# Linear attention and two expert layers on one core: the left pad of SBUF made 32 bytes shorter, and two block differences moved ahead

## The chip, the cores and the metric

The kernel runs on one core of a Trainium2 chip. A core has a matmul engine (PE, with its weight loads shown apart as PEld), a vector engine (DVE), a scalar engine (ACT), a GpSimd engine (POOL) and a sync engine (SP), which here issues nearly all DMAs. They share SBUF, 128 partitions wide; matmuls write to PSUM. The metric is the device time of one execution in microseconds (us), lower is better.

## The reference

```python
kv  = einsum('bhsd,bhse->bhde', k, v)              # B 4, H 8, S 576, D 64
out = einsum('bhsd,bhde->bhse', q, kv)             # linear attention
x   = out / sqrt(mean(out*out, -1) + 1e-6) * g_norm
x   = x.transpose(0, 2, 1, 3).reshape(2304, 512)
h   = x @ w_in                                      # 512 -> 2048
x   = (h * clip(h + 3, 0, 6) / 6) @ w_out           # 2048 -> 512
p   = domain_probs / (domain_probs.sum(-1, keepdims=True) + 1e-9)
y   = sum over e of p[:, e:e+1] * (relu(x @ w1[e]) @ w2[e])     # 4 experts, 512 -> 1024 -> 512
```

All inputs are float32. The weights of the first layer pass through a bit conversion on the way in (lines 144 to 162).

## The kernel before, in words

**Precision.** Matmul operands are float32r. Each float32 value is split into a high part (an ACT copy to float32r) and a low part (a DVE subtraction), and each product is made of three matmuls: high·high, high·low, low·high. Every matmul has a 128x128 stationary operand, loaded just before it.

**Three stages.** First the attention, in eight halves of a batch element. Then stage two, the first layer: 16 column tiles of the hidden dimension in units of 1, 2, 3, 4 and 6 tiles, and for each unit five token blocks, four of 512 tokens and one of 256. `ff_in` makes 12 matmuls that share a PSUM bank, with x as the moving operand (lines 333 to 335; high parts in tiles xh0 to xh4, low parts in xl0 to xl4). ACT and DVE make the activation of it and split it into gH and gL. `ff_out`, three steps behind, makes 12 matmuls with gH or gL as the moving operand (line 356). Four `ff_in` calls are used as filling in the attention already. The sums over units stand in acc.

Then stage three, the four experts, in three passes over 768 tokens each; a pass has 16 quads (4 experts times 4 pairs of hidden tiles). The product x @ w1 is made in 7 instead of 8 block products (Strassen's way), so each quad needs sums and differences of weight blocks (tile `sums`, lines 554 to 559, split into `win`) and each pass needs seven moving tiles xs1 to xs7 of 384 tokens: some are plain pieces of acc, others are differences, made in `st1` and `st2` (line 603) and then split (lines 543 and 544). `quad` makes the products 6, 2, 5, 7, 3, 4 of 6 matmuls each, 384 columns wide (line 656), in two PSUM banks in turn, x and y; the first product of the next quad follows. ACT and DVE take the four results c11, c12, c21, c22 from the banks, and split them with the ReLU into `g2`. c11 and c12 rest in `st1` in between, c22 and c21 in `cs`. `outs` of the quad before makes 36 matmuls, 512 columns wide, with `wout` as the moving and `g2` as the stationary operand (line 630), and DVE adds the result, times the token's probability, to acc2 (lines 644 and 646) after the last quad of an expert.

**What sets the order.** A scheduler of the framework orders each engine's instructions by data dependencies, from the order in which the program issues them; on the chip each engine then runs its own list in order. `ahead`, `side` and `builds` are lists of small pieces of ACT and DVE work that the program issues between matmuls: `ahead` before stage three, `side` between the 36 matmuls of line 630. The pieces of the next pass are split: xs1 goes into `side` of the last quad of a pass, the other six are `builds`, issued in the first quad of the next.

**Where the tiles lie.** Pools are laid out from the left end of SBUF and, with side="right", from the right end. Left: the constants and small tiles up to byte 4960 of a partition, then the left pad (48 float32, 192 bytes), then acc, gH and gL, r, xh3 to xl4, and behind them xh0 to xl2 in stage two, and `sums`, st1, st2 and xs1 to xs6 in stage three (xs3 and xs7 take the places of xh3 and xl3). All of these have sizes that are multiples of 512 bytes, so all start where the first does: at byte 5152, which is 32 more than a multiple of 512. A slice with which a matmul starts is a multiple of 512 bytes into its tile. Right: the right pad, the weight tiles of stage two, raw2, `wout`, `g2` and `win`; they start at multiples of 512 bytes.

Of the kernel before, what the change touches and what calls it, by code (L numbers as in the profile page):

```python
# [17 lines left out]
def kernel(  # L18
# [39 lines left out]
    TH = 384  # L58
# [3 lines left out]
    LAG = 3  # L62
    RATE = (4200, 3000, 2600, 2900, 0)
    FMAX = 3.0e38
    PADL, PADR = 48, 248

    const = ctx.enter_context(tc.tile_pool(name="const", bufs=1))
    sp = ctx.enter_context(tc.tile_pool(name="sp", bufs=1))
# [454 lines left out]
    sums = xsp.tile([P, 4, 2, P], F32, tag="sums", name="sums")  # L523
    st1 = xsp.tile([P, 2, TH], F32, tag="st1", name="st1")
    st2 = xsp.tile([P, 2, TH], F32, tag="st2", name="st2")
# [15 lines left out]
    def split(dst, src):  # L541

        nc.scalar.activation(out=dst[0], in_=src, func=AF.Copy)  # L543
        nc.vector.tensor_tensor(out=dst[1], in0=src, in1=dst[0].bitcast(F32), op=ALU.subtract)  # L544

    def convert_in(k):

        r = raw2[k][:, 0].rearrange("p (c i f) -> p i c f", c=KD, i=2)
        win[k] = w = winp.tile([P, 2, 7, 2, P], F32R, tag="win", name="win")
        a11, a12, a21, a22 = (r[:, i, 2 * c:2 * c + 2, :] for i in range(2) for c in range(2))  # L550
        split([w[:, y, 0:2].rearrange("p m c f -> p (m c) f") for y in range(2)], r[:, 0])
        yield
        split([w[:, y, 2] for y in range(2)], a22)
        nc.vector.tensor_tensor(out=sums[:, 0], in0=a21, in1=a22, op=ALU.add)
        yield
        nc.vector.tensor_tensor(out=sums[:, 1], in0=sums[:, 0], in1=a11, op=ALU.subtract)
        nc.vector.tensor_tensor(out=sums[:, 2], in0=a11, in1=a21, op=ALU.subtract)
        yield
        nc.vector.tensor_tensor(out=sums[:, 3], in0=a12, in1=sums[:, 1], op=ALU.subtract)
        split([w[:, y, 3:5] for y in range(2)], sums[:, 0:2])  # L560
        yield
        split([w[:, y, 5:7] for y in range(2)], sums[:, 2:4])
        yield

    def convert_out(k):

        r = raw2.pop(k)[:, 1].rearrange("p (f d) -> p f d", f=2)
        wout[k] = w = wp.tile(
            [P, 2, 2, DM], F32R, tag=f"w{(NA + len(ftiles) + 2 + k % 2) % NW}", name="wout")
        for f in range(2):  # L570
            split([w[:, f, y] for y in range(2)], r[:, f])
            if f == 1:
                load2(k + 2)
            yield

    def build(p):

        t1, t2 = PASSES[p]

        def pieces(h, c):  # L580
            return [(acc[b][:, 2 * c:2 * c + 2, o:o + n], slice(z, z + n)) for b, o, n, z in h]

        b11, b12, b21, b22 = pieces(t1, 0), pieces(t2, 0), pieces(t1, 1), pieces(t2, 1)

        def new(m):
            pool = xp if m in XSHOME else xsp
            xs[m] = pool.tile([P, 2, 2, TH], F32R, tag=XSHOME.get(m, f"xs{m}"), name=f"xs{m}")
            return xs[m]

        def plain(m, b):  # L590
            x = new(m)
            for s, z in b:
                split([x[:, y, :, z] for y in range(2)], s)

        def summed(m, dst, a, b):

            x = new(m)
            if not isinstance(a, list):
                a = [(a[:, :, z], z) for _, z in b]
            if not isinstance(b, list):  # L600
                b = [(b[:, :, z], z) for _, z in a]
            for (s, z), (s2, _) in zip(a, b):
                nc.vector.tensor_tensor(out=dst[:, :, z], in0=s, in1=s2, op=ALU.subtract)  # L603
            split([x[:, y] for y in range(2)], dst)

        return {
            1: lambda: plain(1, b11),
            5: lambda: summed(5, st1, b12, b11),
            6: lambda: summed(6, st2, b22, st1),
            2: lambda: plain(2, b21),  # L610
            3: lambda: plain(3, b22),
            7: lambda: summed(7, st1, b22, b12),
            4: lambda: summed(4, st1, b21, st2),
        }

    def outs(k):

        p, e, j = quads[k]
        w = wout.pop(k)
        g = g2.pop(k)  # L620
        if j == 0:
            po_t["e"] = [bank_b([P, DM], "po2") for _ in range(NI2)]
        ps = po_t["e"]
        lower, upper = range(NI2 // 2), range(NI2 // 2, NI2)
        for part, f in ((lower, 0), (upper, 0), (upper, 1), (lower, 1)):
            for i in part:
                t, o = divmod(i * P, TH)
                gH, gL = (g[f][:, y, t, o:o + P] for y in range(2))
                for m, (lhsT, y) in enumerate(((gH, 0), (gH, 1), (gL, 0))):
                    nc.tensor.matmul(  # L630
                        ps[i], lhsT=lhsT, rhs=w[:, f, y],
                        start=(j == 0 and f == 0 and m == 0), stop=(j == FP - 1 and f == 1 and m == 2))
                    yield
                if f == 1 and j == FP - 1:
                    finish(p, e, i, ps[i])
# [15 lines left out]
    def product(k, bank, m, first):  # L651
        n = 0
        w = win[k]
        for c in range(2):
            for wy, xy in ((0, 0), (0, 1), (1, 0)):
                nc.tensor.matmul(  # L656
                    bank, lhsT=w[:, wy, AOP[m], c], rhs=xs[m][:, xy, c],
                    start=first and n == 0, stop=n == 5, skip_group_check=True)
                n += 1

    def pair(k):
        return (qa, qb) if k % 2 == 0 else (qb, qa)

    def first_product(k):

        x, y = pair(k)
        product(k, x, 1, True)
        return lambda: nc.scalar.activation(out=y, in_=x, func=AF.Copy)

    def quad(k):  # L670


        x, y = pair(k)
        g2[k] = g = [
            wp.tile([P, 2, 2, TH], F32R, tag=f"w{(NA + len(ftiles) + 4 + 2 * (k % 2) + f) % NW}", name="g2")
            for f in range(2)]
        us = xp.tile([P, 2, TH], F32, tag="xh4", name="us")
        cs = xp.tile([P, 2, TH], F32, tag="xl4", name="cs")
        u2, u4, c22, c21, c11, c12 = (z[:, y] for z in (us, cs, st1) for y in range(2))

        def high(f, t, src, func=AF.Relu):
            nc.scalar.activation(out=g[f][:, 0, t], in_=src, func=func)  # L682

        def low(f, t, src):
            nc.vector.scalar_tensor_tensor(  # L685
                out=g[f][:, 1, t], in0=src, scalar=0.0, in1=g[f][:, 0, t].bitcast(F32),
                op0=ALU.max, op1=ALU.subtract)

        product(k, y, 6, False)
        nc.scalar.activation(out=u2, in_=y, func=AF.Copy)  # L690
        product(k, x, 2, False)
        nc.scalar.activation(out=c11, in_=x, func=AF.Copy)  # L692
        high(0, 0, c11)
        low(0, 0, c11)
        product(k, y, 5, False)
        nc.scalar.activation(out=u4, in_=y, func=AF.Copy)  # L696
        product(k, x, 7, True)
        nc.vector.tensor_tensor(out=c22, in0=x, in1=u4, op=ALU.add)  # L698
        high(1, 1, c22)
        low(1, 1, c22)  # L700
        product(k, y, 3, False)
        nc.scalar.activation(out=c12, in_=y, func=AF.Copy)
        high(0, 1, c12)
        product(k, x, 4, False)
        nc.vector.tensor_tensor(out=c21, in0=x, in1=u2, op=ALU.add)
        low(0, 1, c12)
        high(1, 0, c21)
        low(1, 0, c21)
        win.pop(k)

    def run(g):
        return lambda: next(g, None)
# [2 lines left out]
    load2(0)  # L715
    load2(1)
    first = build(0)
    ahead = [first[m] for m in (1, 5, 6, 2, 4)] + [run(convert_in(0))] * 5 + [run(convert_in(1))] * 5
    for n in range(N3 + 1, NI):
        step(n)  # L720
        if ahead:
# [13 lines left out]
    builds = []  # L735
    for k in range(NQ):
        last_of_pass = k + 1 < NQ and quads[k + 1][0] != quads[k][0]
        ci, co = convert_in(k + 1) if 0 < k and k + 1 < NQ else iter(()), convert_out(k)
        side = builds + [run(co), run(co)] + [run(ci)] * 5
        builds = []  # L740
        if last_of_pass:
            nxt = build(quads[k + 1][0])
            side.append(nxt[1])
            builds = [nxt[m] for m in (5, 6, 2, 7, 3, 4)]
        seed()
        every = -(-NI2 * 6 // len(side))
        for z, _ in enumerate(filler):
            if z % every == every - 1 and side:
                side.pop(0)()
        for x in side:  # L750
            x()
        quad(k)
        if k + 1 < NQ:
            seed = first_product(k + 1)
        filler = outs(k)
# [32 lines left out]
```

## Time and profile before

| | |
|---|---|
| profiled execution | 1240.69 us |
| its span, first to last instruction | 1238.8 us |
| runs | 1242.1, 1431.24 and 4258.09 us, median 1431.24 |
| PE busy | 1219.2 us, 98% of the span |
| DVE, ACT busy | 765.6 and 574.3 us, 62% and 46% |
| DMA | 87.14 MB, 70 GB/s in the mean |
| granted PE clock, mean | 0.997 |

The three runs lie far apart; the profiled execution stands beside the lowest of them, and the trace is of it. Busy time of PE counts each matmul from start to end, and matmuls overlap: what a matmul costs is the distance from its start to the next one's, which the chain of waits and the timeline show.

### The profile page before, as it was taken

Reading aid. Unit: us, or ns where it says so; the run is one execution under the profiler, and the core shown is the slowest. Engines: PE = TensorE matmul, PEld = TensorE weight load, DVE = VectorE, ACT = ScalarE, POOL = GpSimd, SP = SyncE. Lnnn points to the kernel's source line nnn. Section 1 sums busy time; section 2 is a strip of 40 time slices with the busy share of each in tenths; the row PEclk is TensorE's granted clock in tenths of the full one; section 3 lists DMA queues with packets and bytes.
Section 4 is the critical chain, followed back from the end, with each engine's and each line's share of the span. In section 5 each row is a group of like instructions: output and inputs, shape, how many; then the busy total and the mean of one; then the engine's idle time right before and its main releaser. Section 6 shows DMA issues by size and latency. Waiting matters only on the chain.

```text
span 1238.8 us, 17507 instructions
## 1 busy us (share of the span) xinstructions
PE 1219.2 (98%) x7069; PEld 1065.7 (86%) x7069; DVE 765.6 (62%) x1469; ACT 574.3 (46%) x1146; POOL 1.6 (0%) x13
## 2 busy tenths in 40 slices
PE   7899999999999999999999999999999999999998
PEld 5778888888888889999999989999999899999997
DVE  5989996673533555565656586656565866565643
ACT  6778453432422334444444454444444644444442
POOL 0000000000000000000000000000000000000000
PEclk8999999999999999999999999999999999999999
DMA  9812221110010001221122122121111221112101
GB/s 336 261 54 86 69 85 34 36 50 1 27 43 1 1 1 68 69 68 68 69 69 68 69 85 102 69 68 69 66 66 67 77 96 67 66 65 68 67 34 51
DMA packets 60832, 87.14 MB, mean 70 GB/s; under 512 B 5200, under 2 KB 37968, under 8 KB 60752
## 3 DMA queue, kind: packets, MB, share of 16 engines
q1 hardware_dynamic: 60592, 86.03, 20.3%
q8 instruction: 55, 0.90, 0.3%
q14 instruction: 25, 0.20, 0.1%
q10 hardware_dynamic: 160, 0.00, 0.0%
HBM read 81.30 MB, written 4.72 MB: 69 GB/s over the span
## 4 chain that ended last, share of the span: by engine, by line
PE 91%; DVE 5%; DMA 2%; ACT 1%; issue 0%; SPq 0%; ACTq 0%
PE po L630 30%; PE po L356 16%; PE qa L656 14%; PE qb L656 14%; PE ph L333 5%; PE ph L334 5%; PE ph L335 5%; DMA raw<-in_moe_w_out_dram 2%; PE po L247 1%; DVE acc L646 1%; DVE xs L544 1%; DVE st L603 1%; PE px L304 0%; DVE xl L315 0%; DMA qin<-in_q_dram 0%; DVE xt L269 0%
## 5 line engine op out<-in xcount | busy, mean ns | idle before, releaser
L630 PE MATMUL po<-wout,g 128*128 128x512 f32 x1728 | 400.7, 389 | 0.0
L630 PEld LDWEIGHTS po<-wout,g 128*128 128x128 f32 x1728 | 323.8, 188 | 64.1
L656 PE MATMUL qb<-xs,win 128*128 128x384 f32 x1008 | 205.6, 339 | 1.2 <-ACT us L696 1.2
L656 PE MATMUL qa<-xs,win 128*128 128x384 f32 x1008 | 205.4, 339 | 0.1
L356 PE MATMUL po<-gH,w 128*128 128x512 f32 (+1 forms) x640 | 196.2, 372 | 0.0
L656 PEld LDWEIGHTS qb<-xs,win 128*128 128x128 f32 x1008 | 179.5, 188 | 3.8 <-ACT us L696 1.8
L543 ACT ACTIVATE wout<-raw 128x512 fp32r<-128x512 f32 x96 | 55.4, 624 | 274.9 <-PE po L630 274.9
L656 PEld LDWEIGHTS qa<-xs,win 128*128 128x128 f32 x1008 | 179.7, 188 | 2.7 <-ACT st L692 0.4
L544 DVE TENSOR_TENSOR wout<-raw,wout 128x512 fp32r<-128x512 f32 x96 | 62.2, 688 | 159.2 <-ACT wout L543 159.2
L356 PEld LDWEIGHTS po<-gH,w 128*128 128x128 f32 x640 | 116.5, 188 | 23.2
L339 ACT ACTIVATE r<-ph,three 128x512 f32<-128x512 f32 (+1 forms) x80 | 51.6, 645 | 164.3 <-PE ph L335 164.1
L340 DVE SCALAR_TENSOR_TENSOR r<-r,ph 128x512 f32<-128x512 f32 (+1 forms) x80 | 50.6, 632 | 113.8 <-ACT r L339 113.6
L333 PE MATMUL ph<-xh,w 128*128 128x512 f32 (+1 forms) x320 | 119.5, 373 | 0.1
L356 PE MATMUL po<-gL,w 128*128 128x512 f32 (+1 forms) x320 | 119.0, 372 | 0.0
L335 PE MATMUL ph<-xh,w 128*128 128x512 f32 (+1 forms) x320 | 119.0, 372 | 0.0
L334 PE MATMUL ph<-xl,w 128*128 128x512 f32 (+1 forms) x320 | 119.0, 372 | 0.0
L685 DVE SCALAR_TENSOR_TENSOR g<-st,g 128x384 fp32r<-128x384 f32 x96 | 53.5, 558 | 81.9 <-ACT g L682 81.9
L682 ACT ACTIVATE g<-cs 128x384 fp32r<-128x384 f32 x96 | 49.7, 518 | 60.4 <-DVE cs L698 58.2
L333 PEld LDWEIGHTS ph<-xh,w 128*128 128x128 f32 x320 | 60.0, 188 | 12.7 <-DVE r L340 0.5
L685 DVE SCALAR_TENSOR_TENSOR g<-cs,g 128x384 fp32r<-128x384 f32 x96 | 53.3, 555 | 28.1 <-ACT g L682 28.1
L334 PEld LDWEIGHTS ph<-xl,w 128*128 128x128 f32 x320 | 60.0, 188 | 11.8
L356 PEld LDWEIGHTS po<-gL,w 128*128 128x128 f32 x320 | 60.1, 188 | 11.6
(95 smaller groups left out, 1253.1 us busy)
## 6 DMA issues: line engine op xcount, KB each, us to landing
raw<-in_moe_w_dram SPq DMA_DIRECT2D x96, 512.0 KB, 4.2
raw<-in_moe_w_in_dram SPq DMA_DIRECT2D x16, 512.0 KB, 3.6
raw<-in_moe_w_out_dram SPq DMA_DIRECT2D x16, 512.0 KB, 3.6
qin<-in_q_dram SPq DMA_DIRECT2D x8, 576.0 KB, 7.8
kin<-in_k_dram SPq DMA_DIRECT2D x8, 576.0 KB, 5.9
vin<-in_v_dram SPq DMA_DIRECT2D x8, 576.0 KB, 6.8
out_dram<-acc SPq DMA_DIRECT2D x18, 256.0 KB, 2.1
dp<-in_moe_domain_probs_dram SPq DMA_DIRECT2D x1, 36.0 KB, 6.9
```

Source lines behind the costliest of these rows:

```text
L333: nc.tensor.matmul(ph, lhsT=w[:, 0, c, :], rhs=xH[t][:, c, :], start=(c == 0), stop=False)
L334: nc.tensor.matmul(ph, lhsT=w[:, 0, c, :], rhs=xL[t][:, c, :], start=False, stop=False)
L335: nc.tensor.matmul(ph, lhsT=w[:, 1, c, :], rhs=xH[t][:, c, :], start=False, stop=(c == KD - 1))
L339: nc.scalar.activation(out=r, in_=ph, func=AF.Relu, bias=three[:, 0:1])
L340: nc.vector.scalar_tensor_tensor(out=r, in0=r, scalar=6.0, in1=ph, op0=ALU.min, op1=ALU.mult)
L356: nc.tensor.matmul(po_t[u, t][o], lhsT=lhsT, rhs=rhs, start=(f == 0 and m == 0), stop=(f == UF[u] - 1 and m == 2))
L543: nc.scalar.activation(out=dst[0], in_=src, func=AF.Copy)
L544: nc.vector.tensor_tensor(out=dst[1], in0=src, in1=dst[0].bitcast(F32), op=ALU.subtract)
L630: nc.tensor.matmul(ps[i], lhsT=lhsT, rhs=w[:, f, y], start=(j == 0 and f == 0 and m == 0), stop=(j == FP - 1 and f == 1 and m == 2))
L656: nc.tensor.matmul(bank, lhsT=w[:, wy, AOP[m], c], rhs=xs[m][:, xy, c], start=first and n == 0, stop=n == 5, skip_group_check=True)
L682: nc.scalar.activation(out=g[f][:, 0, t], in_=src, func=func)
L685: nc.vector.scalar_tensor_tensor(out=g[f][:, 1, t], in0=src, scalar=0.0, in1=g[f][:, 0, t].bitcast(F32), op0=ALU.max, op1=ALU.subtract)
```

## The change

The left pad shrinks from 48 to 40 float32, from 192 to 160 bytes. Every tile of the left pools behind it moves down by 32 bytes and now starts at a multiple of 512 bytes: acc, gH, gL, r, all xh and xl, us, cs, sums, st1, st2, all xs and acc2. The tiles on the right, the constants and the PSUM banks stay where they were.

c11 and c12 no longer rest in st1 but in the first 3072 bytes of `sums`. So st1 and st2 are free between the builds of one pass and of the next, and the two differences b12 - b11 and b22 - st1 become a piece of their own, number 0. For the first pass it is issued in `ahead` before 5 and 6, for the others in `side` of the last quad of a pass, behind xs1; in `builds` stay the splits of 6 and 5, in this order, and the rest.

```diff
-    PADL, PADR = 48, 248
+    PADL, PADR = 40, 248
...
-        def summed(m, dst, a, b):
-
-            x = new(m)
+        def diff(dst, a, b):
+
...
             for (s, z), (s2, _) in zip(a, b):
                 nc.vector.tensor_tensor(out=dst[:, :, z], in0=s, in1=s2, op=ALU.subtract)
+
+        def whole(m, dst):
+            x = new(m)
             split([x[:, y] for y in range(2)], dst)
+
+        def summed(m, dst, a, b):
+            diff(dst, a, b)
+            whole(m, dst)
 
         return {
             1: lambda: plain(1, b11),
-            5: lambda: summed(5, st1, b12, b11),
-            6: lambda: summed(6, st2, b22, st1),
+            0: lambda: (diff(st1, b12, b11), diff(st2, b22, st1)),
+            5: lambda: whole(5, st1),
+            6: lambda: whole(6, st2),
...
-        u2, u4, c22, c21, c11, c12 = (z[:, y] for z in (us, cs, st1) for y in range(2))
+        cc = sums.rearrange("p a b c -> p (a b c)")[:, :2 * TH].rearrange("p (y n) -> p y n", y=2)
+        u2, u4, c22, c21, c11, c12 = (z[:, y] for z in (us, cs, cc) for y in range(2))
...
-    ahead = [first[m] for m in (1, 5, 6, 2, 4)] + [run(convert_in(0))] * 5 + [run(convert_in(1))] * 5
+    ahead = [first[m] for m in (1, 0, 5, 6, 2, 4)] + [run(convert_in(0))] * 5 + [run(convert_in(1))] * 5
...
-            side.append(nxt[1])
-            builds = [nxt[m] for m in (5, 6, 2, 7, 3, 4)]
+            side += [nxt[1], nxt[0]]
+            builds = [nxt[m] for m in (6, 5, 2, 7, 3, 4)]
```

How this moves instructions is shown at three places. Line numbers of the changed kernel are up to 8 higher: 602 for 603, 690 and 693 for 682 and 685, 698 and 704 for 690 and 696, 700 for 692, 706 for 698, 713 for 705.

**DVE, a quad in the middle of a pass, before** (L685 with st are the low parts of c11 and then c12, L698 makes c22, L705 c21, L554 to L559 the sums of the weight blocks of the next quad but one):

```order
L685 SCALAR_TENSOR_TENSOR g_4770<-st_4161,g_4770 128x384
L698 TENSOR_TENSOR cs<-qb,us 128x384
L685 SCALAR_TENSOR_TENSOR g_4771<-cs,g_4771 128x384
L685 SCALAR_TENSOR_TENSOR g_4770<-st_4161,g_4770 128x384
L705 TENSOR_TENSOR cs<-qb,us 128x384
L544 TENSOR_TENSOR win<-raw_4730,win 128x512
L544 TENSOR_TENSOR win<-raw_4730,win 128x256
L685 SCALAR_TENSOR_TENSOR g_4771<-cs,g_4771 128x384
L544 TENSOR_TENSOR win<-sums,win 128x512 x2
L554 TENSOR_TENSOR sums<-raw_4848 128x256
L557 TENSOR_TENSOR sums<-raw_4848 128x256
```

**The same place now:**

```order
L693 SCALAR_TENSOR_TENSOR g_4770<-sums,g_4770 128x384
L554 TENSOR_TENSOR sums<-raw_4730 128x256
L706 TENSOR_TENSOR cs<-qb,us 128x384
L693 SCALAR_TENSOR_TENSOR g_4771<-cs,g_4771 128x384
L693 SCALAR_TENSOR_TENSOR g_4770<-sums,g_4770 128x384
L713 TENSOR_TENSOR cs<-qb,us 128x384
L544 TENSOR_TENSOR win<-raw_4730,win 128x512
L544 TENSOR_TENSOR win<-raw_4730,win 128x256
L693 SCALAR_TENSOR_TENSOR g_4771<-cs,g_4771 128x384
L556 TENSOR_TENSOR sums<-sums,raw_4730 128x256
L557 TENSOR_TENSOR sums<-raw_4730 128x256
L559 TENSOR_TENSOR sums<-raw_4730,sums 128x256
```

The four operations on `sums` come later: the first stands between c11's low part and c22, the other three behind the quad, since c11 and c12 lie in `sums` until then.

**ACT, at the end of the first pass, before** (win, xs and wout are the high parts of splits; the first us of a quad is u2, the second u4, which frees the bank for product 3):

```order
L543 ACTIVATE wout<-raw_6422 128x512 x2
L690 ACTIVATE us<-qb 128x384
L543 ACTIVATE xs_6564<-st_4161 128x768
L696 ACTIVATE us<-qb 128x384
L692 ACTIVATE st_4161<-qa 128x384
```

**The same place now:**

```order
L543 ACTIVATE wout<-raw_6420 128x512 x2
L698 ACTIVATE us<-qb 128x384
L543 ACTIVATE win<-sums 128x512 x2
L704 ACTIVATE us<-qb 128x384
L700 ACTIVATE sums<-qa 128x384
```

Ahead of u4 stand two splits of `sums` in place of the last split of a difference.

**DVE, near the end of stage two, now** (L372 adds a block to acc, L340 and L342 belong to the activation); the two rows L602 of the second pass stood 250 rows further down before:

```order
L372 TENSOR_TENSOR acc_1627<-po_4265,acc_1627 128x512
L602 TENSOR_TENSOR st_4161<-acc_1627,acc_1566 128x768
L340 SCALAR_TENSOR_TENSOR r<-r,ph 128x256
L602 TENSOR_TENSOR st_4162<-acc_1627,st_4161 128x768
L342 TENSOR_TENSOR gL<-r,gH 128x256
L544 TENSOR_TENSOR wout<-raw_4163,wout 128x512 x2
```

The pair for the third pass moves likewise, from behind the second pass into the second quad of it.

## Rows read from the trace of the kernel before

**Rows 1.** The page: the granted clock of PE in 40 slices.

```profile
PEclk8999999999999999999999999999999999999999
```

**Rows 2.** Chain of waits, one quad of stage three: start us, us, what.

```profile
601.94 8.17 PE po L630 x36
610.11 1.06 PE qb L656 x6
...
617.53 2.51 PE po L630 x11
```

**Rows 3.** Chain of waits, stage two: line 356 on a block of 512 tokens.

```profile
304.93 2.80 PE po L356 x12
307.73 0.24 PE ph L333
```

**Rows 4.** The same chain at other times of stage two, blocks of 512.

```profile
101.93 2.80 PE po L356 x12
...
464.53 2.80 PE po L356 x12
```

**Rows 5.** The same chain: line 356 on the block of 256 tokens.

```profile
475.73 1.40 PE po L356 x12
```

**Rows 6.** Timeline of PE inside line 630: start us, us from first start to last end.

```profile
602.24 7.87 PE L630 MATMUL po<-wout,g 128*128 128x512 f32 x34
```

**Rows 7.** Groups of PE by shape: busy us, mean ns of one | idle before.

```profile
L630 PE MATMUL po<-wout,g 128*128 128x512 f32 x1728 | 400.7, 389 | 0.0
L656 PE MATMUL qb<-xs,win 128*128 128x384 f32 x1008 | 205.6, 339 | 1.2 <-ACT us L696 1.2
...
L356 PE MATMUL po<-gH,w 128*128 128x512 f32 x512 | 171.5, 395 | 0.0
...
L356 PE MATMUL po<-gH,w 128*128 128x256 f32 x128 | 24.7, 279 | 0.0
```

**Rows 8.** Busy time by windows: stretch, its length, PE, PEld, DVE, ACT, POOL.

```profile
180.00:200.00 20.00, 20.00 (x87) 16.05 (x86) 19.41 (x35) 7.69 (x13) 0.00 (x0) 1.00 0.26 79
450.00:480.00 30.00, 30.00 (x185) 26.60 (x184) 13.95 (x25) 11.70 (x22) 0.00 (x0) 1.00 0.09 30
```

**Rows 9.** Chain of waits around the ends of the first and second pass.

```profile
711.09 8.17 PE po L630 x36
...
759.15 8.17 PE po L630 x36
...
961.87 8.17 PE po L630 x36
...
1009.49 8.17 PE po L630 x36
```

**Rows 10.** Timeline at the end of the first pass: DVE, ACT and PE.

```profile
736.39 0.94 DVE L603 TENSOR_TENSOR st<-acc,st 128x768 f32<-128x768 f32 x1
...
738.18 0.49 ACT L696 ACTIVATE us<-qb 128x384 f32<-128x384 f32 x1
...
738.72 1.31 PE L656 MATMUL qb<-xs,win 128*128 128x384 f32 x6 [0.58 <-ACT us L696]
```

**Rows 11.** Timeline of a quad in the middle of a pass: load, low c11, c22.

```profile
753.76 0.37 SPq L534 DMA_DIRECT2D raw<-in_moe_w_dram  x1
...
755.03 0.56 DVE L685 SCALAR_TENSOR_TENSOR g<-st,g 128x384 fp32r<-128x384 f32 x1 [1.30 <-ACT g L682]
...
756.08 0.56 DVE L698 TENSOR_TENSOR cs<-qb,us 128x384 f32<-128x384 f32 x1 [0.49 <-PE qb L656]
```

**Rows 12.** Groups of DVE by shape: busy us, mean ns | idle before.

```profile
L342 DVE TENSOR_TENSOR gL<-r,gH 128x512 fp32r<-128x512 f32 x64 | 44.0, 687 | 15.6 <-ACT gH L341 15.3
...
L162 DVE TENSOR_TENSOR w<-r,w 128x512 fp32r<-128x512 f32 x32 | 21.9, 686 | 2.6 <-ACT w L160 2.5
...
L554 DVE TENSOR_TENSOR sums<-raw 128x256 f32<-128x256 f32 x48 | 20.1, 418 | 1.6 <-DMA raw<-in_moe_w_dram 1.6
```

**Rows 13.** DMA issues: KB each, median us from issue to landing.

```profile
raw<-in_moe_w_dram SPq DMA_DIRECT2D x96, 512.0 KB, 4.2
```

## The prediction

> **What bounds the kernel now.** I read the groups of PE first, then the chain of waits for the distance between matmuls, then the windows and the timeline for what DVE and ACT have in hand. From the end of the attention on the chain is made of matmuls at full clock [rows 1], back to back, so the time is the number of matmuls times their distance, and only PE's rate or a new stall of PE can move it.
>
> The distance is not the same for matmuls of one size. In stage two 12 matmuls of line 356, 512 columns wide, take 2.80 us, 233.3 ns each [rows 3]. The same width in line 630: 34 matmuls run from first start to last end in 7.87 us [rows 6], of which the last one's own duration is 0.389 [rows 7], so 33 distances take 7.48 us, 226.7 ns each. The 6.6 ns show again in the durations, 395 against 389 [rows 7]. The 2.80 stands at 101.93 us and at 464.53 us alike [rows 4], and DVE is nearly full in one such stretch and half idle in another, 19.41 of 20 us and 13.95 of 30 [rows 8]; so it is not DVE's or ACT's traffic that stretches it. What distinguishes the two groups is where the moving operand lies: wout on the right, at a multiple of 512 bytes; gH, gL, xh, xl on the left, 32 bytes past one. The stationary operands are on the right in both.
>
> The other two widths are known only in the shifted place: 1.40 us for 12 of 256 columns, 116.7 ns each [rows 5], and for 384 columns, in a quad, 617.53 - 601.94 = 15.59 us less 8.17 for line 630 leaves 7.42 for 42 products, 176.7 ns [rows 2].
>
> **The change part by part.** *The shift by 32 bytes.* After it all moving operands start as wout does. For 512 columns I take line 630's rate as the price: 6.6 ns less. Stage two has 16 tiles x 4 blocks x 24 = 1536 such matmuls; 48 of them fill the attention, where PE waits for others, so 1488 x 6.6 = 9.8 us. For 256 columns nothing shows the aligned rate. Bounds: no gain, or the whole 6.6 ns; I take line 630's rate per column, 226.7 x 256/512 = 113.4, since the shifted rate scales the same way (233.3/2 = 116.7): 16 x 24 = 384 matmuls x 3.3 = 1.3 us. For 384 columns the same rule gives 170.0, 6.7 ns less; times 42 x 48 = 2016 that is 13.5 us. The lowest bound is no gain, a middle one half (3.3 ns, 6.7 us); I keep the 170.0, because per column this group is the worst of the three shifted ones (0.460 ns against 0.456), so nothing suggests that it gains less. Sum: 24.6 us.
>
> A rule speaks against this term. The Trainium skill, "SBUF — State Buffer", Specifications, has lines of 16 bytes and says that a read pays for each new line; a shift by 32 bytes leaves all starts on such lines and the number of lines unchanged. By the rule this term is 0 and the sum 1240 us; by the rows it is 24.6. The rule does not explain why equal widths differ by 6.6 ns here.
>
> DVE and ACT gain nothing: a subtraction of 512 from left tiles takes 687 ns (gL), from right ones 686 (w) [rows 12].
>
> *Can the faster PE be fed?* In stage two DVE is at its fullest around 180 to 200 us, 19.41 of 20 [rows 8], and PE would want 2.8% more of it. That is 19.41 x 1.029 = 19.97, still under 20, and what DVE makes is wanted three steps later. I cost it at 0; if DVE were really full from 100 to 200 us, at most the gain of that stretch is lost, 100 x 2.8% = 2.8 us. In a quad the banks are emptied in about half a product's time, 0.49 of 1.06 us [rows 10, 2], and stay ahead at 1.02.
>
> *c11 and c12 in sums.* Now four DVE operations of 418 ns [rows 12] on sums must wait for them. The order shows the first, L554, between c11's low part and c22, the other three behind the quad. Before c22 DVE is idle for 0.49 us, waiting for PE [rows 11], so 0.42 fits; c22 itself then has until product 3 is through, another 1.06 - 0.56 = 0.50 us. Cost 0, upper bound 0.42 a quad if the idle time were not there (20 us). The three behind the quad run beside line 630's 8.17 us, with 0.68 + 0.42 + 0.56 + 1.36 us of splits: some 4.3 us in all, done before the next c11 is written. ACT's wait there is not queued ahead of anything that PE needs before its next quad. SP's loads are issued as before.
>
> *The differences moved.* At the end of each pass PE loses a little now: from 711.09 to 759.15 us are 48.06, where three quads would be 3 x 15.59 = 46.77, so 1.3 us; at the second end 1009.49 - 961.87 = 47.62, so 0.85 [rows 9]. The wait is for u4 on ACT (738.18 us), behind a split that waits for a difference on DVE (736.39) [rows 10]. Two differences of 0.95 us leave that stretch per pass end, but the four operations on sums, 4 x 0.42 = 1.7 us, come into it, and in the order u4 now stands behind two splits of sums. I expect the wait to change its name and stay: gain 0.4 us over both ends, between 2.1 (all of it) and -2 (each a us longer). Near the end of stage two the pair stands in front of an activation; DVE has half its time free there [rows 8], 0. The shorter pad's memset is on POOL at the start, 0.
>
> Sum: 24.6 + 0.4 = 25.0, from the profiled execution's 1240.69: **1215.7 us**. The median of the runs, 1431, is far off and is not what the trace explains; the lowest run, 1242.1, is 0.1% above the profiled one.
>
> **The rivals.** *No effect of the place.* The 6.6 ns belong to something else that sets line 630 apart, the side of SBUF or the tile read again and again, and the matmuls keep their distance. For it: no row has a left tile at a multiple of 512. Against: operations, widths and weight loads are the same, and gH is read as often in a row as wout is. Only the 0.4 is left: 1240.3 us. The Trainium skill, "TensorE: Matmul & The Clock Gate", Back-to-back issue gap, gives this case as a rule: the gap follows from the columns alone, 216 ns for 512. No matmul of this trace reaches it, and two distances stand at one width [rows 3, 6]. Chance 0.13.
>
> *The products gain half.* 384 columns at 173.3 ns: 25.0 - 6.8 = 18.2, 1222.5 us. Chance 0.10.
>
> *Slower: L554 blocks c22.* DVE runs its list in order, and L554 now stands ahead of c22, whose bank product 4 needs. It waits for the load of its raw tile. Issued at 753.76 us in one quad [rows 11], used about 17 us later, against 4.2 us from issue to landing [rows 13]; so it decides only if a load takes over 15 us longer than that needs, more than 0.99 us past c22's slot (0.49 + 0.50, less the 0.42 of L554 itself). Each us of PE's wait then costs 46 us; above 0.54 us the kernel is slower than before, at 1 us it takes 1215.7 + 46 = 1262. Against it: DMA moves 70 GB/s in the mean and no load is late in stage three now. Chance 0.03.
>
> *More than line 630 shows.* 256 columns gain the full 6.6 and both pass ends close: 1.3 + 1.7 more, 1212.7 us. Chance 0.04.
>
> **How the numbers follow.** The forecast has 0.70: 1215.7, on its own between 1213.5 and 1218.5 (DVE's 2.8 us, the pass ends). The range takes in the case with more and the one with half: 1211 to 1225, leaving out no effect and slower, 0.16, and a little at the edges. Two per cent is about what a measurement of this kernel can tell from no change, and it lies at 1240.69 x 0.98 = 1215.9, all but on the forecast: a little over half of the 0.70 falls below, some 0.43 with errors to either side even, and all of the 0.04; I add a little because line 630's 8.17 us is 0.01 more than 36 x 226.7, which may be the products' start places too (48 x 0.01 = 0.5 us, not in my sum). Faster 0.50, within 0.47, slower 0.03.
>
> **What would show it.** Line 356's 12 matmuls in 2.72 us in place of 2.80; a quad in 15.30 in place of 15.59, with six products of one bank in 1.02; line 630 still at 8.16; mean durations of 395, 339 and 279 ns down to 389, 332 and 276, and the granted clock as before. c22 starts when PE releases it, and L554 waits for no DMA. At the pass ends a wait of about a us for u4. The forecast is wrong if line 356 stays at 2.80 (no effect), if product rows show 1.04 (half), or if DVE's c22 shows a wait for a DMA in each quad.

## The result: 1229.6 us, half of the forecast gain

The changed kernel takes **1229.6 us** (median of 4 runs, 1228.86 to 1231.45); the kernel before takes 1241.2 us (median of the 15 runs taken beside e1 and e2, 1240.32 to 1243.36). Of the four runs of before that belong to the result, two (1431.24 and 4258.09 us) lie far above all others of this kernel and are left aside. Against the other two, 1242.1 and 1241.37 us, the ratio is 0.9904, 95% interval 0.9881 to 0.9928: faster by 1%, and no change by the 2% bound. The forecast, 1215.7 us, and its range from 1211 to 1225 missed: the profiled execution took 1228.86 us, 11.8 less than the 1240.69 before, where 25.0 were forecast.

**The groups of PE by shape after the change** (busy us, mean ns of one | idle before), which answer to [rows 7]:

```profile
L637 PE MATMUL po<-wout,g 128*128 128x512 f32 x1728 | 402.1, 390 | 0.0
L663 PE MATMUL qb<-xs,win 128*128 128x384 f32 x1008 | 203.3, 336 | 1.2 <-ACT us L704 1.2
...
L356 PE MATMUL po<-gH,w 128*128 128x512 f32 x512 | 168.7, 390 | 0.0
...
L356 PE MATMUL po<-gH,w 128*128 128x256 f32 x128 | 25.2, 283 | 0.0
```

One width did about as forecast (395 to 390 ns, forecast 389). The products fell by 3 ns, not by 7 (339 to 336). The 256 columns grew (279 to 283), and line 637, whose operands had not moved, grew by 1 (389 to 390).

**The chain of waits after the change** (start us, us, what) shows the distances themselves, against [rows 2 to 5]:

```profile
299.84 2.72 PE po L356 x12
...
309.43 2.75 PE po L356 x12
...
464.19 1.44 PE po L356 x12
...
472.61 4.31 PE po L356 x36
...
592.99 8.20 PE po L637 x36
...
608.50 1.62 PE po L637 x7
```

Twelve matmuls of 512 columns take 2.72 us, the forecast's figure, and 2.75 where they stand among matmuls of 256. Twelve of 256 take 1.44 in place of 1.40. A quad takes 608.50 - 592.99 = 15.51 us, 15.53 in the mean of the first pass ((701.51 - 484.08)/14, from the first matmuls of line 637), against 15.59 before and 15.30 forecast.

Now the means over all distances of a kind, before and after. In stage two, 512 columns went from 233.3 to 227.1 ns and 256 columns from 116.7 to 119.5. In the middle of the first pass the products went from 176.7 to 174.5 and line 637 from 227.0 to 227.8. As terms:

| | forecast, us | measured, us |
|---|---|---|
| 512 columns, stage two | 9.8 | 6.25 ns x 1488 = 9.3 |
| 256 columns | 1.3 | -2.8 ns x 384 = -1.1 |
| 384 columns, products | 13.5 | 2.2 ns x 2016 = 4.4 |
| line 637 | 0 | -0.8 ns x 1728 = -1.4 |
| pass ends | 0.4 | 0.15 |
| sum | 25.0 | 11.4 |

The remaining 0.4 us of the 11.8 is not shown to come from any of these. Most of it lies ahead of stage three: its first matmul of 512 columns starts at 484.08 us, 8.54 earlier than the 492.62 before, where the terms of stage two make 8.2. The same start stands at 484.98 us in e1, so 0.4 is within what that part varies from run to run.

**The pass ends**, answering to [rows 9, 10]: the same chain, the waits of PE (total, times, longest), and the timeline of the first end.

```profile
701.67 8.20 PE po L637 x36
...
749.28 8.20 PE po L637 x36
...
951.16 8.20 PE po L637 x36
...
998.74 8.20 PE po L637 x36
```

```profile
PE qb L663 <- ACT us L704: 1.2, 2, 0.6
```

```profile
728.17 0.63 ACT L543 ACTIVATE win<-sums 128x512 fp32r<-128x512 f32 x1 [0.51 <-DVE sums L559]
...
728.73 0.49 ACT L704 ACTIVATE us<-qb 128x384 f32<-128x384 f32 x1
...
729.27 0.79 PE L663 MATMUL qb<-xs,win 128*128 128x384 f32 x3 [0.58 <-ACT us L704]
```

The wait changed its cause and stayed, as forecast: u4 now stands behind a split of sums that waits for line 559 on DVE. The ends take 47.61 and 47.58 us where three quads of 15.53 would be 46.6, so 1.0 each; 1.3 and 0.85 were lost before.

**The order of the sums** costs nothing. In DVE's timeline, which answers to [rows 11], line 554 stands just ahead of c22 (line 706), and neither waits for a DMA (that no quad grew longer by it is shown by e2, below):

```profile
761.31 0.42 DVE L554 TENSOR_TENSOR sums<-raw 128x256 f32<-128x256 f32 x1
761.78 0.56 DVE L706 TENSOR_TENSOR cs<-qa,us 128x384 f32<-128x384 f32 x1
```

### The profile page after: what moved, and what is told of

The parts are those of the page before. It is cut to its first block, busy times and chain, and to the rows that moved or that the text cites. A ratio compares the mean times of both kernels' runs of the same rounds, so it can differ in the third digit from the quotient of the medians.

```text
span 1227.0 us, 17550 instructions
## 1 busy us (share of the span) xinstructions
PE 1206.8 (98%) x7069; PEld 1061.9 (87%) x7069; DVE 771.0 (63%) x1469; ACT 586.6 (48%) x1146; POOL 1.6 (0%) x13
## 4 chain that ended last, share of the span: by engine, by line
PE 93%; DVE 3%; ACT 1%; DMA 1%; issue 0%; SPq 0%
PE po L637 32%; PE po L356 16%; PE qa L663 14%; PE qb L663 14%; PE ph L333 5%; PE ph L334 5%; PE ph L335 5%; PE po L247 1%; DMA raw<-in_moe_w_out_dram 1%; DVE acc L653 1%; DVE xl L315 1%; PE px L304 0%; DVE xt L269 0%; DMA qin<-in_q_dram 0%; DVE ssq L256 0%; ACT xh L314 0%
## 5 line engine op out<-in xcount | busy, mean ns | idle before, releaser
L543 ACT ACTIVATE wout<-raw 128x512 fp32r<-128x512 f32 x96 | 55.4, 625 | 226.6 <-PE po L637 226.6
L356 PE MATMUL po<-gL,w 128*128 128x512 f32 (+1 forms) x320 | 117.9, 369 | 0.0
L340 DVE SCALAR_TENSOR_TENSOR r<-r,ph 128x512 f32<-128x512 f32 (+1 forms) x80 | 50.6, 632 | 105.7 <-ACT r L339 105.5
L693 DVE SCALAR_TENSOR_TENSOR g<-sums,g 128x384 fp32r<-128x384 f32 x96 | 53.5, 558 | 81.4 <-ACT g L690 81.4
L543 ACT ACTIVATE win<-sums 128x512 fp32r<-128x512 f32 x96 | 60.7, 632 | 40.2 <-DVE sums L556 37.7
L693 DVE SCALAR_TENSOR_TENSOR g<-cs,g 128x384 fp32r<-128x384 f32 x96 | 53.3, 555 | 27.2 <-ACT g L690 27.2
```

The lines of the kernel that those rows point to most:

```text
L340: nc.vector.scalar_tensor_tensor(out=r, in0=r, scalar=6.0, in1=ph, op0=ALU.min, op1=ALU.mult)
L356: nc.tensor.matmul(po_t[u, t][o], lhsT=lhsT, rhs=rhs, start=(f == 0 and m == 0), stop=(f == UF[u] - 1 and m == 2))
L693: nc.vector.scalar_tensor_tensor(out=g[f][:, 1, t], in0=src, scalar=0.0, in1=g[f][:, 0, t].bitcast(F32), op0=ALU.max, op1=ALU.subtract)
```

## The experiments

### Which half of the change works?

Theory: the place alone. Rival: the order of the sums. Each half was run by itself.

```diff
 # e1_shift_only, from the kernel before
-    PADL, PADR = 48, 248
+    PADL, PADR = 40, 248
 # e2_diff_only, from the changed kernel
-    PADL, PADR = 40, 248
+    PADL, PADR = 48, 248
```

> The kernel before with the left pad 32 bytes shorter and nothing else: c11 and c12 stay in st1, the differences where they were. Theory A, the place of the moving operand alone makes the change's 12 us, and its price depends on the width (512 columns 6.6 ns less, 384 columns 3.3 less, 256 columns 3.3 more): stage two as in the changed kernel, ratio to before 0.990, about 1229 us; a quad takes 15.44 us if the 0.1 us that the changed kernel's quad has beyond 42 x 173.3 + 36 x 226.7 comes from the new order of sums, and 15.54 if it comes from the place. Theory B, the place gives 25 us as forecast and the new order of sums takes 12 back: 1216 us, ratio 0.980, products at 170.0.

> The changed kernel with the left pad of before: only c11 and c12 in sums and the differences moved. Theory A: within 2 us of before, ratio 0.998 to 1.002, matmuls at 233.3, 176.7 and 116.7 ns, quads of 15.59 us, about 1 us at each end of a pass. Theory B: 12 us slower than before, ratio 1.010, quads of 15.8 us with a wait in each.

The shift alone took 1229.77 us (1229.01 to 1230.96), ratio 0.9904 [0.9889, 0.9919]; the order alone 1241.09 us (1240.40 to 1242.97), ratio 0.9998 [0.9989, 1.0006]. The chain of waits of the shift alone:

```profile
442.99 2.72 PE po L356 x12
...
470.88 1.44 PE po L356 x12
...
485.14 8.20 PE po L630 x36
...
500.65 8.20 PE po L630 x36
```

The chain of the order alone:

```profile
445.36 2.80 PE po L356 x12
...
508.68 8.17 PE po L637 x36
...
524.27 8.17 PE po L637 x36
```

The gain at 512 columns, the loss at 256 and the 8.20 of line 630 all come with the shift, and with the old order of sums a quad takes 500.65 - 485.14 = 15.51 us: it is not the new order that took the rest of the forecast 25 us. With the new order alone the quads stay at 524.27 - 508.68 = 15.59. The order gained 0.4 us at the first pass end (47.66 us against 48.06, by the first matmuls) and nothing at the second; in the time of the kernel that can't be seen.

### What a place costs, by itself

```python
# e3_micro_places: groups of 24; m, s in float32 (the names have bytes)
nc.tensor.matmul(pt, lhsT=sta[:, (i // 2) % 4, s:s + 128], rhs=mov[:, i % 2, m:m + n], ...)
```

> Nothing but matmuls in float32r with a weight load each: groups of 24 in one PSUM bank, of 512, 384 and 256 columns, the moving operand 0 to 496 bytes past a multiple of 512, the stationary operand at a multiple or 32, 256 or 480 past one; the layers themselves are left out. Theory A: at 0 past for both, distances of 226.7, 173.3 and 120.0 ns, 13.3 above the columns at 2.4 GHz at each width; at 32 past 233.3, 176.7 and 116.7. If the price goes by the distance of the two operands' places and not by the place of the moving one, both operands shifted alike give the figures of 0 past. The rival that ACT's and DVE's traffic makes the difference: all distances alike here, whatever the place.

The timeline of PE (us from the first start to the last end of a group; c512m32s0b means 512 columns, the moving operand 32 and the stationary 0 bytes past a multiple of 512):

```profile
23.73 5.60 PE L34 MATMUL c512m0s0b<-mov,sta 128*128 128x512 f32 x24
29.17 5.72 PE L34 MATMUL c512m16s0b<-mov,sta 128*128 128x512 f32 x24
34.73 5.77 PE L34 MATMUL c512m32s0b<-mov,sta 128*128 128x512 f32 x24
...
90.35 4.32 PE L34 MATMUL c384m0s0b<-mov,sta 128*128 128x384 f32 x24
...
98.72 4.33 PE L34 MATMUL c384m32s0b<-mov,sta 128*128 128x384 f32 x24
...
140.59 3.04 PE L34 MATMUL c256m0s0b<-mov,sta 128*128 128x256 f32 x24
...
146.32 2.97 PE L34 MATMUL c256m32s0b<-mov,sta 128*128 128x256 f32 x24
149.13 2.89 PE L34 MATMUL c256m64s0b<-mov,sta 128*128 128x256 f32 x24
...
180.04 5.63 PE L34 MATMUL c512m32s32b<-mov,sta 128*128 128x512 f32 x24
```

A row less one duration, over 23, is the distance: (5.60 - 0.39)/23 = 226.5 ns. From the ninth matmul of a group on, with the two places alike, the means are 226.6, 173.3 and 119.9 ns. The differences between widths are 53.3 and 53.4 ns for 128 columns, so a matmul pays **0.417 ns a column and 13.3 ns beside them**. Not "per column", then: no group of 384 columns reached 170.0 (the least was 173.3), and 256 columns stand at 119.9, above the 116.9 that the shifted place gives and the 113.3 at 64 bytes. With both operands shifted by 32 bytes, 512 columns take 226.7 again: it is the place of one against the other that counts.

Beside these matmuls DVE does nothing and ACT makes a copy of 8 columns behind each group, and the places still differ: the rival, traffic of ACT and DVE, falls. Theory A failed at one figure. With the moving operand at 32 bytes, 512 and 256 columns take 233.1 and 116.9 ns, as expected, but 384 columns take 173.3, not 176.7. The same offset made the other way (moving at 0, stationary at 480 bytes) gave 176.8. So the place alone does not settle the distance; the next experiments come back to this.

### Where the other 0.1 us of a quad is

At 226.7 and 173.3 ns a quad would take 36 x 226.7 + 42 x 173.3 ns = 15.44 us; it takes 15.53.

```python
# e4_micro_switch: 42 narrow, then 36 wide, three times for each set of places a, b, s
nc.tensor.matmul(pa[i // 6 % 2], lhsT=sta[:, i // 2 % 4, s:s + 128], rhs=mov[:, i % 2, a:a + 384], ...)
nc.tensor.matmul(pb[i // 3 % 6], lhsT=sta[:, i // 2 % 4, s:s + 128], rhs=mov[:, i % 2, b:b + 512], ...)
```

> Matmuls alone, no work of the other engines beside them: three quads' worth in a row (42 of 384 columns, then 36 of 512) for each of eleven places of the moving operand of the 384, of the 512 and of the stationary operand; the kernel's own computation is left out. Question: a quad of the changed kernel takes 15.54 us, while 42 x 173.3 + 36 x 226.7 ns is 15.44. Theory A: the 0.1 us comes from the switch between the two widths itself, so the pattern with all places alike takes 15.54 here too, all three shifted by 64 bytes takes the same 15.54, and the 384 shifted by 32 bytes takes the 15.59 of the kernel before. Rival: the 0.1 us comes from the traffic of DVE and ACT; then the pattern with all places alike takes 15.44. For the other places of the 384 the steady distances of e3_micro_places give, by A, 15.54 where 173.3 ns stood (64, 192, 256, 320 bytes) and 15.65 where 176 ns stood (128, 448 bytes).

The timeline of PE (nm32w0s0e are the 42 narrow ones of the set with the narrow at 32 bytes, the wide and the stationary at 0; wm32w0s0e the 36 wide ones of the same set):

```profile
40.10 7.47 PE L50 MATMUL nm0w0s0e<-mov,sta 128*128 128x384 f32 x42
47.41 8.36 PE L54 MATMUL wm0w0s0e<-mov,sta 128*128 128x512 f32 x36
55.61 7.47 PE L50 MATMUL nm0w0s0e<-mov,sta 128*128 128x384 f32 x42
...
86.71 7.58 PE L50 MATMUL nm32w0s0e<-mov,sta 128*128 128x384 f32 x42
94.13 8.34 PE L54 MATMUL wm32w0s0e<-mov,sta 128*128 128x512 f32 x36
102.30 7.58 PE L50 MATMUL nm32w0s0e<-mov,sta 128*128 128x384 f32 x42
...
133.35 7.44 PE L50 MATMUL nm64w0s0e<-mov,sta 128*128 128x384 f32 x42
...
148.80 7.44 PE L50 MATMUL nm64w0s0e<-mov,sta 128*128 128x384 f32 x42
```

From start to start a set takes 55.61 - 40.10 = 15.51 us with all places alike, 15.59 with the narrow ones at 32 bytes (the quad before), and 15.45 at 64 bytes. No other engine works beside them, so the rival falls: with all places alike, 0.07 of the 0.1 us is here without it. The distances are 173.3 and 226.8 ns from the ninth matmul of each run on, so the 0.07 lies just behind the switches of width. The other 0.02 of the kernel's 15.53 stays open. And the wide matmuls, whose own places did not change, take 8.20 or 8.17 us according to where the narrow ones lay. Theory A was right on the cause and wrong in detail: its 15.54 came out as 15.51; for 64 and 192 bytes it had 15.54 where 15.45 and 15.58 were measured, and for 128 and 448 bytes 15.65 where 15.55 and 15.58 were. So a steady distance doesn't tell what a mixture takes. The set that the expectation calls all three shifted had in fact the stationary operand left at 0 (both widths at 64 bytes against it); it gave 15.52, with 8.24 for the wide ones. The shift of both sides is tried in the kernel, next.

### The same in the kernel

```diff
 # e6_both_sides_32
-    PADL, PADR = 40, 248
+    PADL, PADR = 48, 240
 # e7_products_at_32 (xs3 and xs7 likewise, as a slice from element 8 on)
+    xsp.tile([P, 8], F32, tag="shift", name="shift")
 # e5_narrow_at_64 (xh4 and xl4 likewise)
-        gH = gp.tile([P, TB], F32R, tag="gH", name="gH")[:, :n]
+        z = OFF if n < TB else 0          # OFF = 16
+        gH = gp.tile([P, TB], F32R, tag="gH", name="gH")[:, z:z + n]
```

> The changed kernel with the left pad at its old length and the right pad 32 bytes shorter, so that both sides start 32 bytes past a multiple of 512: no moving operand is on a multiple of 512 any more, but each lies to its stationary operand as in the changed kernel. Theory A (the place of one operand against the other counts): as the changed kernel, 1229.6 us, quads of 15.54, 512 columns at 226.7 ns. Rival (the multiple of 512 itself counts, as the prediction had it): 512 columns back to 233.3 ns in both stages, so 9.9 us in stage two and another 1728 x 6.7 ns = 11.5 us in line 637: 1251 us, or 1241 if line 637 keeps its rate.

> The changed kernel with only xs1 to xs7, the moving operands of the 384-wide products, back at 32 bytes past a multiple of 512. Theory A: only the quads go back, from 15.54 to 15.59 us, 48 x 0.058 = 2.8 us: 1232.4 us; stage two as in the changed kernel, first line-637 start at 484.2 us. The prediction's price (6.7 ns a product): 13.5 us, 1243.1. The half that the micro kernel's steady 173.3 ns against 176.7 gives: 6.7 us, 1236.3.

> The changed kernel with only the moving operands of the block of 256 tokens (xh4, xl4 and the slices of gH and gL) shifted by 64 bytes; everything else is where it was. Theory A (a matmul's distance follows from where the moving operand lies against the stationary one, for each width on its own): 256 columns take 113.3 ns in place of 120.0, 384 x 6.7 ns = 2.6 us less, 1227.0 us; a run of 36 of line 356 in 4.08 us in place of 4.31. Rival (the 3.3 ns that 256 columns lost come from their neighbours, the matmuls of 512 columns or the activation that must be ready): no change, 1229.6 us and 4.31.

Both sides at 32 bytes took 1229.28 us (1228.93 to 1229.88), ratio 0.9900 [0.9886, 0.9913], as the changed kernel, with no matmul operand of stages two and three at a multiple of 512. Its chain:

```profile
442.88 2.72 PE po L356 x12
...
485.06 8.20 PE po L637 x36
```

The products back at 32 bytes took 1232.26 us (1231.74 to 1235.03, ratio 0.9922 [0.9908, 0.9936]), on theory A's 1232.4, far from the 1243.1 of the prediction's price and from the 1236.3 of the steady distances. Its chain shows quads of 503.28 - 487.68 = 15.60, and line 642 (637 there) back from 8.20 to 8.17 although none of its operands moved:

```profile
487.68 8.18 PE po L642 x36
...
503.28 8.17 PE po L642 x36
```

The trace is of the slowest of the five runs, 1235.03 us. Its first matmul of line 642 starts at 487.52 us, where 484.2 was expected; this stands beside a lower granted clock in the attention, 0.83 in the mean between 20 and 40 us and 0.91 between 80 and 100, against 0.91 and 1.00 in the trace of the changed kernel. The quads come later, at full clock.

The 256 columns at 64 bytes took 1228.73 us (1228.12 to 1229.31, ratio 0.9895 [0.9881, 0.9908]), where theory A had 1227.0 and the rival 1229.6; the runs overlap with those of the changed kernel, so the distances have to tell. Its chain:

```profile
469.24 1.41 PE po L365 x12
...
471.89 4.24 PE po L365 x36
```

36 matmuls take 4.24 us, 118 ns each, not the 113.3 of the small kernel. All distances of 256 columns have a mean of 118.0 ns against 119.5. So neither theory held: the place helped the distances, but by a quarter of what the steady figure promised.

### A second look at places, and at the stationary operand

> Matmuls alone again, the kernel's own computation left out. First part: 24 matmuls of 256 columns after 36 of 512, and 42 of 384 after 36 of 512, with the narrower ones' moving operand at twelve and eleven places, the 512 always at 0. e5_narrow_at_64 had 118 ns for 256 columns at 64 bytes, where e3_micro_places had 113.3 after other matmuls of 256. Theory A2 (the place sets which rhythms are possible, and the matmuls before decide which one it falls into): 256 at 64 bytes after 512 takes 118 here too, 256 at 0 takes 119.5, and no place needs to show the 113.3; theory A (place alone): 113.3 at 64 bytes. Second part: groups of 24 with a stationary operand of 128 or of 64 columns, at moving places 0, 32 and 64. Theory W (what a matmul pays beyond its columns, and what the place changes, is the reading of the next stationary operand beside the moving one): with 64 columns the 13.3 ns halve, 512 columns take 220 ns, 384 take 166.7, 256 take 113.3 at place 0, and the places differ by less than 3.4 ns. Rival (a fixed cost of a matmul's start that has nothing to do with the stationary operand): the same figures with 64 columns as with 128, 226.7 and 233.3, 173.3, 120 and 116.9.

```python
# e8_micro_fine, first part as e4 with (256 or 384 columns, place a) before the 36 wide; second part:
nc.tensor.matmul(pt, lhsT=sta[:, (i // 2) % 4, 0:cols], rhs=mov[:, i % 2, m:m + n], ...)
```

The timeline of PE (nm64e: narrow at 64 bytes behind 36 wide; c512m32s64k: 512 columns at 32 bytes, stationary of 64 columns):

```profile
80.30 2.96 PE L50 MATMUL nm32e<-mov,sta 128*128 128x256 f32 x24
...
124.41 2.99 PE L50 MATMUL nm64e<-mov,sta 128*128 128x256 f32 x24
...
631.33 5.60 PE L61 MATMUL c512m0s128k<-mov,sta 128*128 128x512 f32 x24
...
636.99 5.73 PE L61 MATMUL c512m0s64k<-mov,sta 128*64 128x512 f32 x24
...
648.72 5.74 PE L61 MATMUL c512m32s64k<-mov,sta 128*64 128x512 f32 x24
```

Behind 512 columns, 256 columns at 64 bytes take 117.9 ns a piece (start of the group to start of the next), as in the kernel; the best of the twelve places are 32 and 288 bytes, 116.8, and none shows 113.3. That is theory A2: the same matmuls have several steady rhythms (113.3 ns in e3, 117.9 here and 117.7 in the second part, for the same group of 24 as in e3 behind others), and what ran before them is what differs. Theory W held in part. With 64 columns of weights the place matters less (512 columns from the ninth on: 229.3 at 0 and 230.7 ns at 32 bytes, against 226.7 and 233.3), so the size of the stationary operand has to do with it; that it is the load of the weights is not shown. The 13.3 ns did not halve: 512 columns at 0 took more and not the 220 that W wanted, 384 columns still took 173.3, and only 256 columns fell to W's 113.3. What makes the 13.3 ns stays open.

### Better places

> The changed kernel with only xs1 to xs7, the moving operands of the 384-wide products, 64 bytes past a multiple of 512. In e4_micro_switch the pattern of a quad took 15.454 us with the products there against 15.507 with all alike. Theory A2: the matmuls of the kernel fall into the same rhythm, a quad takes 15.48 in place of 15.54, 48 x 0.053 = 2.5 us: 1227.1 us. Rival (in the kernel the first product, the copies and the waits at the pass ends set another rhythm, as they did for 256 columns): no change, 1229.6.

> The changed kernel with the moving operands of each width at the best place that e4_micro_switch and e8_micro_fine showed between matmuls of 512 columns: xs1 to xs7 (384 columns) 64 bytes past a multiple of 512, the block of 256 tokens 32 bytes past it, all of 512 columns on it. Theory A2: the quads of e9_products_at_64, 15.455 us, and 116.8 ns for 256 columns in place of 119.5, 384 x 2.7 ns = 1.0 us: 1226.84 - 1.0 = 1225.8 us, the first start of line 637 at 483.0 us or a little later. Rival (the rhythm of 256 columns depends on more than the place and its neighbours' width, as at 64 bytes, where it kept 118): 1226.8.

```diff
 # e9_products_at_64: as e7, with 16 in place of 8 elements
+    xsp.tile([P, 16], F32, tag="shift", name="shift")
 # e10_combined: e9, and as e5 with
+    OFF = 8
```

The products at 64 bytes took 1226.84 us (1225.29 to 1228.35), ratio 0.9884 [0.9867, 0.9900], below all runs of the changed kernel, and near theory A2's 1227.1. Its chain: 15.45 us a quad, as in the small kernel, and 8.17 for the line that is 637 in the changed one:

```profile
499.45 8.17 PE po L642 x36
...
514.90 8.17 PE po L642 x36
```

The last one, with 256 columns back at 32 bytes, took 1226.18 us (1225.02 to 1227.68), ratio 0.9877 [0.9860, 0.9893]. Its chain has the 1.40 of before again, and 512 columns keep their 2.72:

```profile
447.43 2.72 PE po L365 x12
...
469.59 1.40 PE po L365 x12
```

All its distances of 256 columns have a mean of 116.8 ns against 119.5, as theory A2 had it, so the 1.0 us is there in the distances; in the time, 0.7 us below the run before (1225.8 was expected), it lies inside the spread.

## Why the prediction was wrong

**The mechanism was right in the main.** The matmuls bound the kernel, their distance depends on where the moving operand lies, the shift moves it, and DVE and ACT kept up. 512 columns gave 9.3 us of the 9.8, line 356's twelve came to 2.72, and e1 and e2 put the gain on the shift.

**The step that failed is the price of the other widths**: "line 630's rate per column", 113.4 ns for 256 and 170.0 for 384 columns. Its reason was that the shifted distances scale with the columns (233.3/2 = 116.7; 0.460 ns a column for 384). That was a coincidence of one place. With alike places the distances are 0.417 ns a column and 13.3 ns more (e3), so 384 columns could gain 3.3 ns at most and 256 columns had 3.3 to lose. The rival "half" (1222.5 us) had the right steady price for 384 columns, 173.3, with a chance of 0.10. For 256 columns the bounds "no gain, or the whole 6.6 ns" had no loss in them, though no row excluded one.

**A second term was missing**: matmuls of two widths in turn disturb each other. It took 1.2 ns more of each product than the steady 173.3 and 0.8 ns of each matmul of line 637, which was costed at nothing because its operands stay: 2016 x 1.2 + 1728 x 0.8 ns = 3.8 us. Of the 13.6 us between forecast and measured terms, the price of 384 columns makes 6.8 (13.5 less 3.3 ns x 2016), this 3.8, the 256 columns 2.4, and the rest 0.6. The prediction had the sign of it in hand, line 630's 8.17 against 36 x 226.7 = 8.16, and took it for 0.5 us to win; e4 and e7 showed that this 8.17 becomes 8.20 when the products move.

**Not 512 bytes.** The prediction took the multiple of 512 for the cause. e6 has none in stages two and three and is as fast: what counts is the distance between the moving and the stationary operand.

**Right:** the order of the sums and L554 cost nothing, the wait for u4 took another cause and stayed, and the pair of differences was worth 0.4 us by itself (e2), 0.15 with the faster quads.

**A slip that cost nothing.** In the rival "slower", 17 us from issue to use less 4.2 to landing is 12.8, and 0.49 + 0.50 less 0.42 is 0.57 and not 0.99: a load had 13.4 us to spare by these figures, not 15. None of the 48 of line 554 waited for a DMA after the change.

**The two rules weighed.** The Trainium skill, "SBUF — State Buffer", Specifications, has reads pay by lines of 16 bytes, by which the shift was worth 0; the shift alone was worth 11.4 us (e1), and in e3 even 16 bytes turned 226.6 into 231.4 ns. The Trainium skill, "TensorE: Matmul & The Clock Gate", Back-to-back issue gap, gives some 216 ns for 512 columns, from the columns alone, as the gap of a single matmul by itself. For a stream of weight loads and matmuls, which this kernel is, the same section of the Trainium skill has both set the spacing, and some 131 ns at 512 columns; the prediction left this out. No run here comes down to either: 226.6 was the least steady distance of 512 columns, and 233.3 stood at the same width. The form of the first rule, though, so much a column and a fixed part, is that of e3: the trace agrees with 0.417 ns a column, and has 13.3 ns where the rule has 2.5. Weighed for its form and not for its 216 ns, it spoke against the per-column price.

## What to carry to other kernels

A distance known at one width is not a rate: take two widths at the same place before scaling to a third, and keep a loss in the bounds where none is excluded. Where matmuls bound a kernel, the offset between moving and stationary operand is worth trying, but the figure has to be taken from the kernel's own mixture of widths, since the steady distance of one width promised 113.3 ns where 118 came. A change of places can also slow instructions whose operands did not move.

## What the runs showed of the hardware

- With the two operands alike, float32r matmuls with a 128x128 stationary operand loaded for each stand 226.6, 173.3 and 119.9 ns apart for 512, 384 and 256 columns; moving the one against the other changed this by -6.6 to +6.7 ns in e3.
- 256 bytes between the two operands are the same as 0: 226.7, 173.3 and 120.0 ns in e3. That does not make every pair of places 256 bytes apart alike: 256 columns took 113.3 ns at 64 and 117.7 at 320 bytes there.
- The first five to seven matmuls after a change of width or place are often irregular (512 columns at 256 bytes in e3: 226, 235, 229, 233 and 231 ns, then 226.6 in the mean), and the same matmuls can settle at different distances: 384 columns at 32 bytes at 173.3 ns in e3, behind 384 at 16 bytes, and at 176.6 in e8, behind a smaller stationary operand.
